# A Fourier filter and a snake MLP on one core: the DFT tables moved into the GpSimd DMA queue, and a weight scaled in eight parts

## Chip, cores and metric

The kernel runs on one core of a Trainium2 chip. The metric is the device time of one execution in microseconds (us). The profile comes from one execution that the hardware profiler recorded; its times are counted from the start of the span.

## What is computed

The input x has 8 batches of 3008 rows by 256 channels. Along the 3008 rows of each batch a real Fourier transform is taken, multiplied with a complex filter, and transformed back. The result goes through an MLP with 2048 hidden channels and the snake activation.

```python
def _attn_ref(x, filt_r, filt_i):
    X = np.fft.rfft(x, axis=1)
    F = (filt_r + 1j * filt_i)[None, :, :]
    Y = X * F
    y = np.fft.irfft(Y, n=x.shape[1], axis=1)
    return y.astype(np.float32)

def _moe_ref(x, w_in, w_out, alpha):      # x: (8 * 3008, 256)
    h = x @ w_in
    s = np.sin(alpha * h)
    g = h + s * s / (alpha + 1e-09)
    return (g @ w_out).astype(np.float32)
```

## The kernel before

The transform of length 3008 = 47 x 64 is done with matrix products, in two steps. Step one is a DFT of length 47, for which 24 frequencies (NK) are kept; step two is a DFT over the 64 residues, folded by symmetry, with one matrix for each of the 24 frequencies. The matrices are constants in device memory. The forward table of step two is `wb` (128 rows by 24 x 128 columns, fp16, 768 KB), the backward tables are `wg` and, with its row halves exchanged and one negated, `wgs` (the same size each). They are cut into chunks of eight frequencies, that is 1024 columns or 256 KB; `s0` = 0, 8, 16 names a chunk.

The program has a prologue and a main loop. The main loop runs over 47 groups `g` of 512 rows of the MLP. In each group, for eight slots `q`, `mlp_in` (L269) makes two blocks of hidden channels (a matrix product, then a sine on ScalarE), `mlp_out` (L283) does a part of the second product of the group before, and `square` (L279) squares the sines on VectorE. The transform of the later batches, 1 to 7, is cut into small pieces that a plan by slots (L413 to 457, `at(slot, f, ...)`) puts between the MLP's pieces: `f1` (step one, result `asb`), `f2x`, `product` with the filter, `f2g` and `f3` (back). Their rearrangements between the steps go through device memory, by DMAs issued on SP.

The prologue does the transform of batch 0, before any MLP work can start, and keeps it on the chip. Its order is written out by hand (L487 to 506):

- `f1_chip` (L151) is step one on the x of batch 0, which arrives in four parts, and `turn1` (L162) turns its result into `bint`;
- `f2x(0, t)` (L201), for t = 0 to 11, multiplies two frequencies each with `wb`;
- `fold_filter(s0, 8)` (L405) copies a chunk of the loaded filter on VectorE to the other half of the partitions;
- `product(0, k, 0)` (L210), for k = 0 to 5, multiplies four frequencies with the filter's real and imaginary parts on VectorE, giving `z` and `t2`, in two buffers each;
- `g_chip(k, half)` (L172) multiplies `z` with `wg` and `t2` with `wgs` on TensorE; k = 0, 1 need chunk 0, k = 2, 3 chunk 8, k = 4, 5 chunk 16;
- `turn2` (L183) and `f3` (L249) finish batch 0; then the first `mlp_in` can start.

`keep_busy(n, zero)` (L388) issues n matrix products whose result is not used. `prep_w_out` (L351) makes `w_out2` out of the loaded `w_out16`: sixteen blocks of 256 columns, each multiplied on VectorE with 1/alpha. The plan has it in four parts of four blocks in slots 6, 8, 10 and 12; `mlp_out` of group 0 reads the result from slot 8 on.

The loads of the prologue stand in two queues. GpSimd's queue holds the loads that also cast fp32 to fp16: x of batch 0 (eight DMAs), the three filter chunks (four DMAs each), w_in (four), x of batch 1 (eight, once `bint` is no longer read, since both share a buffer), and w_out (two). SP's queue holds the tables: a first part of `wb` at once, the rest of `wb` behind the third part of x, and each chunk of `wg` and `wgs` behind the filter chunk that the products ahead of it need. These dependencies are made by `gate` (L123), which makes one DMA's issue wait for an earlier DMA to land.

Of the kernel before, what the change touches and what calls it, by code (L numbers as in the profile page):

```python
# [9 lines left out]
FP16 = mybir.dt.float16  # L10
# [5 lines left out]
MT, R, NK, RP = 47, 64, 24, 32  # L16
# [48 lines left out]
def kernel(  # L65
# [10 lines left out]
    nc = tc.nc  # L76
# [3 lines left out]
    def dram(ap, off, dims):  # L80
        return bass.AP(tensor=ap.tensor, offset=ap.offset + off, ap=dims)
# [3 lines left out]
    wb_d = nc.inline_tensor(wb_np, name="wb_tbl")  # L85
    wg_d = nc.inline_tensor(wg_np, name="wg_tbl")
# [3 lines left out]
    wgs_d = nc.inline_tensor(wgs_np, name="wgs_tbl")  # L90
# [7 lines left out]
    ginpool = ctx.enter_context(tc.tile_pool(name="ginp", bufs=2))  # L98
# [13 lines left out]
    wb = cpool.tile([128, NK * 128], FP16, name="wb")  # L112
    wg = cpool.tile([128, NK * 128], FP16, name="wg")
# [6 lines left out]
    xt, asb, scr1, bint, xs, z, t2, gsb, scr2, gin, yt, vt, po, ot, x_dma, w_in_dma, filter_dma = (  # L120
        {} for _ in range(17))

    def gate(ins, earlier):  # L123

        tc.add_manual_dep(ins.ins, earlier.ins.name, mybir.DependencyInfo(
            mybir.DependencyClass.Sync, mybir.DependencyReason.DATA), reason="order of transfers")

    def load_x(b, parts=2):

        xt[b] = (xbpool if b else vpool).tile([GT, RP, C], FP16, name="xt", tag="xb" if b else "vt")  # L130
        n = RP // parts
        for h in range(parts):
            for p0, p1 in ((0, 80), (80, GT)):
                x_dma[b, h] = nc.gpsimd.dma_start(  # L134
                    out=xt[b][p0:p1, n * h:n * h + n, :],
                    in_=dram(x, (b * S + RP * p0 + n * h) * C, [[RP * C, p1 - p0], [1, n * C]]))
# [203 lines left out]
    def prep_alpha():  # L340
        ps = pso.tile([128, 2, C], FP32, name="psal", tag="po")
        nc.tensor.matmul(out=ps[:, 0, 0:16], lhsT=alpha_r, rhs=ident32, start=True, stop=True)
        nc.vector.tensor_copy(out=alpha_t, in_=ps[:, 0, 0:16])
        nc.vector.tensor_scalar(out=recip, in0=alpha_t, scalar1=1e-9, scalar2=None, op0=ALU.add)
        nc.vector.reciprocal(out=recip, in_=recip)
# [3 lines left out]
                                   in_=moe_w_out[1024 * h:1024 * h + 1024, :].rearrange("(b p) c -> p b c", p=128))  # L349

    def prep_w_out(k):  # L351
        for i in range(4 * k, 4 * k + 4):
            nc.vector.tensor_scalar(out=w_out2[:, i, :], in0=w_out16[:, i, :],  # L353
                                    scalar1=recip[:, i:i + 1], scalar2=None, op0=ALU.mult)

# [32 lines left out]
    def keep_busy(n, src):  # L388

        ps = psh.tile([128, 2, C], FP32, name="idle", tag="ph")  # L390
        for _ in range(n):
            nc.tensor.matmul(out=ps, lhsT=ident[0:src.shape[0]], rhs=src, start=True, stop=True)

    def load_filter(s0, n, earlier=None):

        for f, src in ((0, filt_r), (1, filt_i)):
            first = nc.gpsimd.dma_start(out=fri[0:32, f, s0:s0 + n, :],
                                        in_=dram(src, s0 * C, [[MT * C, 32], [C, n], [1, C]]))
            if earlier is not None and f == 0:
                gate(first, earlier)  # L400
            filter_dma[s0, f] = nc.gpsimd.dma_start(
                out=fri[32:64, f, s0:s0 + n, :],
                in_=dram(src, (MT - s0) * C, [[MT * C, 32], [-C, n], [1, C]]))
# [11 lines left out]
    def at(slot, f, *args):  # L415
        plan.setdefault(int(2 * slot), []).append((f, args))
# [19 lines left out]
    for g in range(NCH - 1):  # L436
# [4 lines left out]
        slots = (4, 6) if len(todo) == 2 else (3, 4, 6, 7) if g == 4 else (3, 4, 5, 6)  # L441
        for q, u in zip(slots, todo):
            at(8 * g + q, f3, *u)
    for k in range(4):
        at(6 + 2 * k, prep_w_out, k)
    for k in range(2):
        at(13, prep_m, k)
    at(14, load_w_in32, 0)
# [10 lines left out]
    with tc.manual_schedule():  # L459
        nc.sync.dma_start(out=wa2, in_=wa2_d.ap())  # L460
        nc.sync.dma_start(out=ident, in_=id_d.ap())
        nc.scalar.dma_start(out=alpha_r, in_=moe_alpha.rearrange("(a p) -> a p", p=128))
        nc.scalar.dma_start(out=ident32, in_=id32_d.ap())
        nc.scalar.dma_start(out=we2, in_=we2_d.ap())
        nc.scalar.dma_start(out=wa, in_=wa_d.ap())
        nc.scalar.dma_start(out=we, in_=we_d.ap())
        nc.sync.dma_start(out=wb[:, 0:8 * 128], in_=wb_d.ap()[:, 0:8 * 128])
        zero = cpool.tile([128, 512], FP16, name="zero")
        nc.vector.memset(zero, 0.0)
        warm = cpool.tile([128, 1], FP32, name="warm")  # L470
        nc.vector.memset(warm, 0.0)
        nc.scalar.activation(out=warm, in_=warm, func=AFT.Sin)
        load_x(0, 4)
        for s0 in (0, 8, 16):
            load_filter(s0, 8, None if s0 else x_dma[0, 1])
        for h in range(2):
            hs = slice(1024 * h, 1024 * h + 1024)
            for cb in range(2):
                w_in_dma[h, cb] = nc.gpsimd.dma_start(out=w_in16[:, cb, hs],
                                                      in_=moe_w_in[128 * cb:128 * cb + 128, hs])  # L480
        wgs = ginpool.tile([128, NK * 128], FP16, name="wgs", tag="gin")
        gate(nc.sync.dma_start(out=wb[:, 8 * 128:], in_=wb_d.ap()[:, 8 * 128:]), x_dma[0, 2])
        for s0 in (0, 8, 16):
            cs = slice(128 * s0, 128 * s0 + 1024)
            gate(nc.sync.dma_start(out=wg[:, cs], in_=wg_d.ap()[:, cs]), filter_dma[s0, 0])
            nc.sync.dma_start(out=wgs[:, cs], in_=wgs_d.ap()[:, cs])
        a_c = vpool.tile([128, 2, NK, 128], FP16, name="a_c", tag="vt")  # L487
        prep_alpha()
        keep_busy(8, zero)
        for k in range(8):  # L490
            f1_chip(k)
            if k % 2:
                keep_busy(2 if k < 7 else 1, zero)
        bint[0] = xbpool.tile([128, NK, C], FP16, name="bint", tag="xb")
        b_c = agpool.tile([128, 2, RP, NK, 4], FP16, name="b_c", tag="ag")
        for f, *args in (
                (turn1, 0), (turn1, 1), (turn1, 2), (f2x, 0, 0), (turn1, 3), (turn1, 4), (f2x, 0, 1),
                (turn1, 5), (turn1, 6), (f2x, 0, 2), (turn1, 7), (fold_filter, 0, 8), (turn1, 8),
                (f2x, 0, 3), (product, 0, 0, 0), (turn1, 9), (f2x, 0, 4), (turn1, 10), (f2x, 0, 5),
                (product, 0, 1, 0), (turn1, 11), (f2x, 0, 6), (keep_busy, 2, zero), (g_chip, 0, 0), (g_chip, 0, 1), (f2x, 0, 7),  # L500
                (fold_filter, 8, 8), (f2x, 0, 8), (keep_busy, 2, zero), (product, 0, 2, 0), (g_chip, 1, 0), (g_chip, 1, 1),
                (f2x, 0, 9), (keep_busy, 2, zero), (product, 0, 3, 0), (f2x, 0, 10), (f2x, 0, 11), (keep_busy, 2, zero), (g_chip, 2, 0), (g_chip, 2, 1),
                (fold_filter, 16, 8), (keep_busy, 2, zero), (product, 0, 4, 0), (g_chip, 3, 0), (g_chip, 3, 1),
                (product, 0, 5, 0), (keep_busy, 2, zero), (g_chip, 4, 0), (g_chip, 4, 1), (keep_busy, 2, zero), (g_chip, 5, 0), (g_chip, 5, 1),
                (keep_busy, 1, zero)):
            f(*args)
        gin[0] = ginpool.tile([4 * NK, RP, C], FP16, name="gin", tag="gin")
        for j in range(4):
            turn2(j)
        load_x(1, 4)  # L510
        load_w_out(0)
        load_w_out(1)
        for i in range(4):
            if i % 2 == 0:
                keep_busy(1, zero)
            f3(i // 2, i % 2)

        for g in range(NCH):
            for q in range(8):
                if g and q == 7:  # L520
                    evict_out(g - 1, 0)
                mlp_in(g, 2 * q)
                if g:
                    mlp_out(g - 1, q, 1)
                for f, args in plan.get(16 * g + 2 * q, ()):
                    f(*args)
                mlp_in(g, 2 * q + 1)
                if g:
                    mlp_out(g - 1, q, 0)
                for f, args in plan.get(16 * g + 2 * q + 1, ()):  # L530
                    f(*args)
                if g and q == 7:
                    evict_out(g - 1, 1)
                    store_out(g - 1, 0, 4, (nc.sync,))
                if q % 2:
                    square(g, q)
        out_last(NCH - 1)
# [28 lines left out]
```

## Time and profile before

| | us |
|---|---|
| median of 3 runs | 833.29 |
| lowest, highest | 833.17, 837.02 |
| the profiled execution | 836.87 |
| its span, first to last instruction | 835.0 |
| last matmul of `g_chip` (L177) starts | 38.35 |
| first matmul of `mlp_in` (L274) | 42.2 |

The parts of the page, for the main loop, by engine and line, costliest first (line, engine, operation, count; then busy time, and mean ns of one; then the idle time before them and what ended it):

```profile
L276 ACT ACTIVATE vt<-ph 128x512 f16<-128x512 f32 x688 | 404.5, 601 | 141.8 <-PE ph L274 136.9
L293 PE MATMUL po<-w_out,vt 128*128 128x256 f16 x2944 | 426.5, 272 | 1.1 <-DVE w_out L353 0.6
L274 PE MATMUL ph<-yt,w_ina 128*128 128x512 f16 x1376 | 399.4, 379 | 0.0
```

How to read the profile: PE is TensorE, PEld its weight loads, DVE is VectorE, ACT is ScalarE, POOL is GpSimd and SP is SyncE; a q behind the name is that engine's queue of instructions. `L177` is line 177 of the kernel. A transfer is shown by the instruction that issues it and by what waits for its landing; the time in between is in the chain of waits as a piece of DMA. The whole main loop is one where TensorE works without a break and ScalarE waits for it.

### The profile page before, as it was taken

The numbers are of one execution on the slowest core, as the hardware profiler recorded it, in microseconds if no ns is written. First come the engines' busy times: TensorE is split into PE (matmuls) and PEld (weight loads), VectorE is DVE, ScalarE is ACT, GpSimd is POOL, SyncE is SP. The second block draws the span as 40 slices with busy tenths as digits, with TensorE's granted clock in tenths as the row PEclk, the third lists the DMA queues.
The fourth block names the chain that finished last, engine by engine and source line by source line (L and its number), as shares of the span: only waits on it lengthen the run. The fifth ranks groups of instructions, "written<-read, shape, count | busy, mean of one in ns | idle before, by whom it ended". The sixth has DMA issues, their size and how long they took to land.

```text
span 835.0 us, 15131 instructions
## 1 busy us (share of the span) xinstructions
PE 816.3 (98%) x6242; PEld 573.1 (69%) x6242; DVE 509.9 (61%) x675; ACT 619.0 (74%) x1156; POOL 35.0 (4%) x65
## 2 busy tenths in 40 slices
PE   7699999999999999999999999999999999999997
PEld 4557776677767776677767776677766777766666
DVE  4586976676466665566655684567655775444442
ACT  5596987787777777788777887777877787766663
POOL 5400000000000000000000000000000000000000
PEclk9999999999999999999999999999999999999999
DMA  9946365424543164612834146331645123310111
GB/s 198 210 75 215 120 169 127 141 76 107 145 107 122 51 156 95 202 31 72 191 99 140 51 105 172 101 102 51 160 118 142 61 93 95 67 51 26 26 52 51
DMA packets 67829, 91.28 MB, mean 109 GB/s; under 512 B 5512, under 2 KB 52376, under 8 KB 66248
## 3 DMA queue, kind: packets, MB, share of 16 engines
q1 hardware_dynamic: 59664, 70.99, 29.5%
q0 software_dynamic: 7568, 19.14, 11.8%
q8 instruction: 49, 0.80, 0.4%
q10 hardware_dynamic: 528, 0.18, 0.1%
q14 instruction: 20, 0.16, 0.1%
HBM read 59.62 MB, written 46.66 MB: 127 GB/s over the span
## 4 chain that ended last, share of the span: by engine, by line
PE 91%; DMA 3%; DVE 3%; ACT 1%; POOL 1%; issue 0%; SPq 0%; POOLq 0%; DVEq 0%
PE po L293 42%; PE ph L274 37%; PE psa L143 3%; PE psy L262 3%; PE psg L234 2%; PE psx L204 2%; DMA fri<-in_filt_r_dram 1%; DMA wgs<-wgs_tbl 1%; PE pe L307 1%; DMA xt<-in_x_dram 1%; DVE vt L281 1%; PE psm L372 0%; ACT vt L276 0%; DVE gin L191 0%; DVE w_ina L385 0%
## 5 line engine op out<-in xcount | busy, mean ns | idle before, releaser
L276 ACT ACTIVATE vt<-ph 128x512 f16<-128x512 f32 x688 | 404.5, 601 | 141.8 <-PE ph L274 136.9
L293 PE MATMUL po<-w_out,vt 128*128 128x256 f16 x2944 | 426.5, 272 | 1.1 <-DVE w_out L353 0.6
L293 PEld LDWEIGHTS <-vt 128*128 128x128 f16 x2944 | 287.4, 98 | 172.2 <-issue 1.1
L274 PE MATMUL ph<-yt,w_ina 128*128 128x512 f16 x1376 | 399.4, 379 | 0.0
L281 DVE TENSOR_TENSOR vt<-vt 128x2048 f16<-128x2048 f16 x188 | 230.1, 1224 | 195.3 <-ACT vt L276 194.4
L274 PEld LDWEIGHTS <-w_ina 128*128 128x128 f16 x1376 | 128.2, 98 | 32.6
L318 DVE COPY ot<-po 128x512 f32<-128x512 f32 x92 | 62.9, 688 | 22.2 <-PE po L293 21.3
L208 ACT CAST xs<-psx 128x512 f16<-128x512 f32 x96 | 56.8, 596 | 7.6 <-PE psx L204 7.4
L144 DVE CAST asb<-psa 96x512 f16<-96x512 f32 x56 | 38.3, 685 | 33.4 <-PE psa L143 30.6
L236 ACT CAST gsb<-psg 128x512 f16<-128x512 f32 x84 | 49.5, 589 | 11.5 <-PE psg L234 10.7
L293 PE MATMUL po<-m_t,yt 128*128 128x256 f16 x368 | 55.2, 273 | 0.0
L267 DVE CAST yt<-psy 128x240 f16<-128x240 f32 (+45 forms) x92 | 32.2, 351 | 32.8 <-ACT yt L264 31.6
L264 ACT CAST yt<-psy 128x376 f16<-128x376 f32 (+46 forms) x127 | 45.9, 362 | 7.5 <-PE psy L262 0.6
L276 ACT ACTIVATE vt<-ph,alpha_t 128x512 f16<-128x512 f32 x64 | 43.7, 703 | 9.4 <-PE ph L274 9.3
L262 PE MATMUL psy<-we,gin 96*128 96x94 f16 x512 | 42.1, 204 | 0.0
L134 POOL DMA_DIRECT2D xt<-in_x_dram x40 | 21.3, 540 | 491.8 <-PE psy L262 300.7
L262 PEld LDWEIGHTS <-gin 96*128 96x128 f16 x512 | 35.6, 97 | 6.9 <-issue 0.5
L293 PEld LDWEIGHTS <-yt 128*128 128x128 f16 x368 | 36.0, 98 | 4.2
L144 ACT CAST asb<-psa 96x512 f16<-96x512 f32 x56 | 32.9, 587 | 8.0 <-PE psa L143 7.7
L217 DVE TENSOR_TENSOR z<-xs,fri 128x1024 f16<-128x1024 f16 x48 | 33.0, 687 | 8.3 <-ACT xs L208 4.6
L274 PE MATMUL ph<-yt,w_in 128*128 128x512 f16 x128 | 37.8, 379 | 0.2 <-ACT yt L264 0.2
L204 PE MATMUL psx<-bint,wb 128*128 128x256 f16 x192 | 36.8, 276 | 0.4 <-ACT bint L169 0.2
(69 smaller groups left out, 383.7 us busy)
## 6 DMA issues: line engine op xcount, KB each, us to landing
scr<-asb SPq DMA_DIRECT2D x14, 768.0 KB
bint<-scr SPq DMA_DIRECT2D x21, 512.0 KB
scr<-gsb SPq DMA_DIRECT2D x21, 512.0 KB
out_dram<-ot SPq DMA_DIRECT2D x31, 320.0 KB
xt<-in_x_dram POOLq DMA_DIRECT2D x12, 640.0 KB, 7.7
gin<-scr SPq DMA_DIRECT2D x7, 768.0 KB
out_dram<-ot SPq DMA_DIRECT2D x16, 256.0 KB
gin<-scr SPq DMA_DIRECT2D x7, 576.0 KB
```

Of the source, the lines that this page charges most:

```text
L144: (nc.vector.tensor_copy if u % 2 else nc.scalar.copy)(out=asb[b][:, 2 * u:2 * u + 2, :], in_=ps)
L204: nc.tensor.matmul(out=ps[:, i, :], lhsT=wb[:, 128 * (2 * t + i):128 * (2 * t + i) + 128], rhs=bint[b][:, 2 * t + i, :], start=True, stop= ...
L208: nc.scalar.copy(out=xs[b, t // 2][:, t % 2 * 2:t % 2 * 2 + 2, :], in_=ps)
L217: nc.vector.tensor_tensor(out=z[k], in0=xs[b, k], in1=fri[:, 0, k4, :], op=ALU.mult)
L236: nc.scalar.copy(out=gsb[b][:, 2 * t:2 * t + 2, :], in_=ps)
L262: nc.tensor.matmul(out=ps[:, t, :], lhsT=gin[b][:, 4 * a + t, 128 * cb:128 * cb + 128], rhs=we if b else we2, start=True, stop=True)
L264: (nc.vector.tensor_copy if G == 0 and cb else nc.scalar.copy)(out=yt[g][:, cb, :, lo:lo + n], in_=ps[:, :, 0:n])
L274: nc.tensor.matmul(out=ph, lhsT=(w_in16 if g < 4 else w_ina)[:, cb, 128 * jb:128 * jb + 128], rhs=yt[g][:, cb], start=(cb == 0), stop=(cb ...
L276: nc.scalar.activation(out=vt[g][:, jb, :], in_=ph, func=AFT.Sin, scale=alpha_t[:, jb:jb + 1] if g < 4 else 1.0)
L281: nc.vector.tensor_tensor(out=v4, in0=v4, in1=v4, op=ALU.mult)
L293: nc.tensor.matmul(out=po[g, h][:, i, :], lhsT=vt[g][:, k, ts] if k < 16 else yt[g][:, k - 16, t], rhs=w_out2[:, k, :] if k < 16 else m_t[ ...
L318: nc.vector.tensor_copy(out=ot[g][:, 2 * h:2 * h + 2, :], in_=po[g, h])
```

## The change

The seven table loads on SP and their gates go. The same loads are issued by GpSimd instead, between the filter chunks: behind filter chunk 0 the rest of `wb` and the chunk 0 of `wg` and `wgs`, behind chunks 8 and 16 their `wg` and `wgs`. The loads of w_in come after all of these. The first part of `wb` stays on SP. `prep_w_out` is cut into eight parts of two blocks in slots 6, 6.75, 7.5 and so on to 11.25. One of the two idle matrix products ahead of `g_chip(5, ...)` goes.

```diff
     def prep_w_out(k):
-        for i in range(4 * k, 4 * k + 4):
+        for i in range(2 * k, 2 * k + 2):
             nc.vector.tensor_scalar(out=w_out2[:, i, :], in0=w_out16[:, i, :],
                                     scalar1=recip[:, i:i + 1], scalar2=None, op0=ALU.mult)
...
-    for k in range(4):
-        at(6 + 2 * k, prep_w_out, k)
+    for k in range(8):
+        at(6 + 0.75 * k, prep_w_out, k)
...
         load_x(0, 4)
+        wgs = ginpool.tile([128, NK * 128], FP16, name="wgs", tag="gin")
         for s0 in (0, 8, 16):
+            cs = slice(128 * s0, 128 * s0 + 1024)
             load_filter(s0, 8, None if s0 else x_dma[0, 1])
+            if s0 == 0:
+                nc.gpsimd.dma_start(out=wb[:, 8 * 128:], in_=wb_d.ap()[:, 8 * 128:])
+            nc.gpsimd.dma_start(out=wg[:, cs], in_=wg_d.ap()[:, cs])
+            nc.gpsimd.dma_start(out=wgs[:, cs], in_=wgs_d.ap()[:, cs])
         for h in range(2):
             hs = slice(1024 * h, 1024 * h + 1024)
             for cb in range(2):
                 w_in_dma[h, cb] = nc.gpsimd.dma_start(out=w_in16[:, cb, hs],
                                                       in_=moe_w_in[128 * cb:128 * cb + 128, hs])
-        wgs = ginpool.tile([128, NK * 128], FP16, name="wgs", tag="gin")
-        gate(nc.sync.dma_start(out=wb[:, 8 * 128:], in_=wb_d.ap()[:, 8 * 128:]), x_dma[0, 2])
-        for s0 in (0, 8, 16):
-            cs = slice(128 * s0, 128 * s0 + 1024)
-            gate(nc.sync.dma_start(out=wg[:, cs], in_=wg_d.ap()[:, cs]), filter_dma[s0, 0])
-            nc.sync.dma_start(out=wgs[:, cs], in_=wgs_d.ap()[:, cs])
...
-                (product, 0, 5, 0), (keep_busy, 2, zero), (g_chip, 4, 0), (g_chip, 4, 1), (keep_busy, 2, zero), (g_chip, 5, 0), (g_chip, 5, 1),
+                (product, 0, 5, 0), (keep_busy, 2, zero), (g_chip, 4, 0), (g_chip, 4, 1), (keep_busy, 1, zero), (g_chip, 5, 0), (g_chip, 5, 1),
```

## The prediction

> **What bounds the kernel now.** The page's first part says that TensorE is busy nearly throughout:
>
> ```profile
> PE 816.3 (98%) x6242; PEld 573.1 (69%) x6242; DVE 509.9 (61%) x675; ACT 619.0 (74%) x1156; POOL 35.0 (4%) x65
> ```
>
> So only a stretch in which it waits can give time back. The list of who waited for whom, cut to 0 to 90 us, finds those waits:
>
> ```profile
> PE psg L177 <- DMA wgs<-wgs_tbl: 4.8, 3, 1.9
> ...
> PE psg L177 <- DMA wg<-wg_tbl: 1.4, 2, 1.0
> ...
> PE po L293 <- DVE w_out L353: 0.6, 1, 0.6
> ```
>
> The columns are total, times and longest, in us. The backward tables cost 6.2 us of TensorE's own waiting, all in g_chip. The chain of waits between 14 and 45 us, in order of time (start, length, what), says why they are late:
>
> ```profile
> 14.44 10.77 DMA fri<-in_filt_r_dram
> ...
> 25.23 0.32 SPq L485
> 25.55 0.05 issue
> 25.60 10.61 DMA wgs<-wgs_tbl
> 36.20 0.04 issue
> 36.24 1.00 PE psg L177 x15
> 37.24 0.43 PE idle L392 x2
> 37.67 0.91 PE psg L177 x16
> 38.58 0.02 issue
> 38.61 0.70 DVE b_c L180
> ```
>
> The last pair of tables is issued only when the third filter chunk has landed (25.21), and needs 10.6 us for 256 KB. The table of stretches tells what it shares the DMA engines with (second column from the right: DMA share, last: GB/s):
>
> ```profile
> 0.00:12.00 12.00, 8.56 (x64) 4.73 (x64) 3.54 (x11) 3.99 (x8) 6.99 (x17) 1.00 0.85 166
> 12.00:24.00 12.00, 7.95 (x92) 6.01 (x91) 8.05 (x14) 8.55 (x18) 6.18 (x11) 0.97 1.18 227
> 24.00:30.00 6.00, 5.35 (x43) 3.74 (x41) 4.75 (x6) 4.69 (x9) 1.93 (x2) 0.78 1.03 209
> 30.00:36.00 6.00, 2.81 (x36) 2.22 (x36) 2.81 (x5) 2.15 (x4) 3.94 (x8) 1.00 1.09 247
> 36.00:45.00 9.00, 7.77 (x90) 5.56 (x90) 5.12 (x9) 5.34 (x11) 1.83 (x2) 1.00 1.23 189
> 45.00:50.00 5.00, 4.49 (x38) 2.78 (x38) 3.90 (x6) 4.52 (x8) 0.00 (x0) 1.00 0.20 27
> ```
>
> From 12 to 45 us the DMA engines are full. So what sets the prologue is the order in which bytes are moved: w_in (20.8 to 24.1) and x of batch 1 (from 29.25) are issued while the last tables are still outstanding, though nobody needs them before 42.2 and 50.7. From 50 us on DMA is idle until 58. GB/s times length gives bytes moved: 1.99 MB by 12 us, 4.72 by 24, 5.97 by 30, 7.45 by 36, 9.15 by 45.
>
> **The tables.** Seven SP issues and their two kinds of gate go; SP's next work is the store at 58.21, so nothing is queued behind them. GpSimd gets seven issues more. Its x issues take a mean 540 ns, so 7 x 0.54 = 3.8 us, in a queue that waits 4.0 us ahead of the filter, 2.1 and 2.0 inside it and 4.0 before x of batch 1: hidden as long as eight DMAs are under way, since the built program lets each GpSimd DMA wait for the one eight before it. Then the order in the queue alone counts. From issue sizes (x 1504 KB, the first part of wb, small loads: 1.93 MB together; every step after that 512 KB or 0.524 MB) the running sum after each step, and when the curve above reaches it: filter 0 2.45 MB; wb rest 2.98, 16.4 us; pair 0 3.50, 18.6; filter 8 4.03, 21.0; pair 8 4.55, 23.3; filter 16 5.08, 25.7; pair 16 5.60, 28.2; w_in first half 6.12, 30.6; second 6.65, 32.8; x of batch 1 8.19, 39.9; w_out 9.24, 45.5. From last byte to waiter I add 1.5 us, an estimate: x (1.93 MB) is passed before 12 us and its last matmul started at 13.08.
>
> Against the needs: wb at 17.9 (it came at 18.84). Pair 0 at 20.1; TensorE stood ready at 21.47 and 22.07, its first g_chip began in earnest at 23.2, so 1.1 us come back there. Filter 8 at 22.5; VectorE reaches its fold after the second product, 23.2, not 23.94. Pair 8 at 24.8, before TensorE gets there. Filter 16 at 27.2: this is late next, since VectorE would reach its fold after product 3 at about 27.3 (29.00 before, less the 1.6 that g_chip(1) gains). Call the start of this fold F. Behind it stand products 4 and 5, then g_chip(5). From the rows of the trace: fold to product 1.35 (23.94 to 25.29), two products 2.63 (32.59 to 34.54+0.68), then 0.04 and a last g_chip 1.06 (37.51 to 38.35+0.22). The last ends at F + 5.1 = 32.4, against 38.57. Pair 16 at 29.7 is ahead of g_chip(4) at about F + 2.7 = 30.0. Gain 6.2.
>
> What is moved back: w_in's halves land at 32.1 and 34.3; the first mlp_in moves from 42.2 to 36. x of batch 1 is complete at 41.4, first used at 44.5. The first half of w_out (8.72 MB) lands near 44, first scaling 49.9. No wait is added if the curve holds.
>
> It need not hold: it was made by two queues. The nearest row of one queue alone is 36 to 45 us, when SP's tables are in: 189 GB/s. Then filter 16 lands at 12 + 3.09/0.189 + 1.5 = 29.8 and the last g_chip ends at 34.9: gain 3.7. That row is x and w_out with casting, w_out in short rows, while the tables are plain copies in long rows; so I take the curve, and keep 3.7 as the low end. The high end is VectorE's own pace: F one microsecond earlier, 7.2.
>
> [...]
>
> **The scaling of w_out.** Still 16 operations of 0.86/4 = 0.21 us, so VectorE's total is the same; they come in twos and are done by slot 11.25, not 12. TensorE's waits around it are 0.59 (at 70.03, the last scaling) and 0.27 (at 57.60, for asb behind four scalings): the gain is at most 0.86. But four scalings now come ahead of the square at 63.04, which pushes it and two asb copies back by up to 0.86, where VectorE's idle time is 0.57: a loss is possible up to about the same. I take 0.4 gained, with -0.9 to +0.9 kept.
>
> **keep_busy.** One matmul of 0.22 fewer before g_chip(5). It lies under the wait for product 5 (g_chip(4) ends a microsecond after F + 2.7, the product comes at F + 4.0), so nothing; 0.2 gained without that cover.
>
> **The sum.** 6.2 + 0.4 = 6.6 off the profiled execution, whose 836.87 (span 835.0) is 3.6 above the median of 833.29. TensorE's granted clock was 0.998 and steady, and after 50 us DMA has slack, so the excess may well lie in the prologue's transfers, and then an ordinary run has less waiting to give. All of it there: gain 3.0, 830.3. None: 826.7. I take the middle: 4.8 gained, **828.5**, own range 826 to 830.5.
>
> **Rivals.** (a) *One queue feeds more slowly.* For: 189 GB/s in the only stretch with GpSimd alone. Against: 204 GB/s at 3 to 6 us with hardly anything beside it, and short rows. Gain 3.7 + 0.4 - 1.8 = 2.3: 831.0, within 0.5%. Chance 0.20.
>
> (b) *The wait is not there in an ordinary run*, since the tables mostly come in time, and VectorE's chain sets the end anyway: gain about the 0.4 of w_out, 832.9. For: two of three runs are 3.6 shorter than the profile. Against: even then 3 of the 6.6 are left. Chance 0.10.
>
> (c) *Slower: GpSimd cannot keep its queue full.* Filter 16 must land after 33.5 for F + 5.1 to pass 38.57, which is 3.09 MB in 20 us: below 155 GB/s the change loses. For: two issues beside VectorE's fold took twice their time:
>
> ```profile
> 19.57 1.21 POOL L401 DMA_DIRECT2D fri<-in_filt_i_dram  x1 [1.96 <-DMA fri<-in_filt_i_dram]
> 20.76 0.56 POOL L479 DMA_DIRECT2D w_in<-in_moe_w_in_dram  x1
> ...
> 24.10 1.18 POOL L479 DMA_DIRECT2D w_in<-in_moe_w_in_dram  x1 [0.33 <-DMA fri<-in_filt_i_dram]
> ```
>
> Both end when the fold does (19.40 + 1.22; 23.94 + 1.22). Against: three folds at 0.6 each are 1.9 us in 20, and eight DMAs (over 1 MB) cover them; the slowest 3 us of the queue alone still moved 164 GB/s (39 to 42). At 135 GB/s the last g_chip ends at F = 36.4 + 5.1 = 41.5, 2.9 late, and half of w_out lands at 63.4 where 59.0 is needed: 4.4, less VectorE's 1.4 of idle time. 833.3 + 5.9 = 839. Chance 0.10.
>
> [...]
>
> (d) *The scaling takes back its 0.9* while the tables give their share: 6.2 - 1.8 - 0.9 = 3.5, 829.8. Chance 0.07.
>
> **Chances and range.** The forecast has 0.53. 0.5% is 4.2 us, about what a measurement of this kernel can tell: faster is below 829.1. The forecast lies there for most of its range; together with gains above it 0.56. (a), (b), (d) and the rest of the forecast are no change: 0.33. Slower: 0.11. The range must hold the forecast, the full 7.2 + 0.9 and (a), (b), (d): 825 to 834; outside is (c).
>
> **What will show it.** In the profile of the changed kernel: wgs no longer in the chain of waits; the third fold starts near 27 and waits for the filter's DMA or not at all; the last psg ends near 32 to 33 (38.57 before); the first mlp_in near 36, without a wait for w_in; no wait at L353. The prediction is wrong if filter 16 lands after 30, if a gap of DMA shows between 12 and 30 us (queue starved), if w_in or w_out is waited for, or if asb waits grow between 50 and 65 us by more than the two waits that go.

## The result, and the profile after

The changed kernel took 830.23 us in the median of 15 runs (828.98 to 833.54), the kernel before 834.73 us in the median of 15 (832.81 to 839.18). The ratio is 0.9947, 95% interval 0.9931 to 0.9962: 4.5 us, half a percent, faster. The forecast was 828.5 us and a gain of 4.8.

The profiled execution of the changed kernel took 829.13 us, with a span of 827.2, against 836.87 and 835.0. These two differ by more than the medians do; why is shown below.

Who waited for whom on TensorE, 0 to 90 us, in the changed kernel (total, times, longest, in us), the list's head:

```profile
PE psal L342 <- DMA ident<-id_tbl: 3.1, 1, 3.1
PE psa L156 <- DMA xt<-in_x_dram: 1.1, 2, 0.6
PE psg L177 <- DVE t L219: 0.7, 2, 0.4
```

The waits for wg and wgs, 6.2 us before, are gone, and so is the one for the scaling of w_out; g_chip now waits only for VectorE's product. `psal` and `psa` in this list belong to the start and to step one. VectorE's own order of time in the changed kernel (start, length, instruction, and in brackets the idle time before it):

```profile
25.67 0.68 DVE L219 TENSOR_TENSOR t<-xs,fri 128x1024 f16<-128x1024 f16 x1
26.40 1.22 DVE L407 COPY fri<-fri 64x4096 f16<-64x4096 f16 x1
27.76 0.69 DVE L217 TENSOR_TENSOR z<-xs,fri 128x1024 f16<-128x1024 f16 x1
...
29.57 0.69 DVE L219 TENSOR_TENSOR t<-xs,fri 128x1024 f16<-128x1024 f16 x1
31.36 0.69 DVE L180 CAST b_c<-psg 128x512 f16<-128x512 f32 x1 [1.11 <-PE psg L177]
```

The third fold starts the moment VectorE has finished the product ahead of it, without a wait for the filter. What sets the end of the prologue in this profile is VectorE's chain; in the two later profiles of the changed kernel the third fold waited for the filter, by 1.56 and 0.30 us. The last matmul of g_chip starts at 31.11 (38.35 before), the first mlp_in at 34.99 (42.23 before). The table of stretches of the changed kernel (third column from the right: granted TensorE clock; then DMA share and GB/s):

```profile
12.00:24.00 12.00, 10.13 (x123) 7.61 (x122) 9.57 (x15) 10.21 (x22) 8.86 (x16) 1.00 1.16 251
24.00:30.00 6.00, 5.46 (x64) 3.97 (x62) 5.82 (x9) 5.16 (x11) 5.12 (x8) 1.00 1.10 214
30.00:36.00 6.00, 5.26 (x66) 3.70 (x64) 3.65 (x8) 3.73 (x9) 2.34 (x4) 1.00 1.09 213
36.00:45.00 9.00, 8.23 (x68) 4.97 (x66) 7.88 (x11) 7.84 (x15) 1.04 (x2) 1.00 1.23 189
45.00:50.00 5.00, 5.00 (x36) 2.69 (x35) 4.74 (x11) 5.00 (x11) 0.00 (x0) 1.00 0.03 4
```

In this profile one queue alone moved 251 GB/s from 12 to 24 us, where two moved 227 before; two later profiles of the changed kernel have 212 and 246. The bytes are the same and are done at nearly the same time, about 45 us; their order is another.

### The profile page after: what moved, and what is told of

It reads as the page before. It is cut to its first block, busy times and chain, and to the rows that moved or that the text cites. A ratio compares the mean times of both kernels' runs of the same rounds, so it can differ in the third digit from the quotient of the medians.

```text
span 827.2 us, 15124 instructions
## 1 busy us (share of the span) xinstructions
PE 814.4 (98%) x6241; PEld 570.7 (69%) x6241; DVE 509.7 (62%) x675; ACT 618.3 (75%) x1156; POOL 38.6 (5%) x72
## 4 chain that ended last, share of the span: by engine, by line
PE 88%; DVE 2%; DMA 1%; ACT 0%; issue 0%; DVEq 0%
PE po L293 42%; PE ph L274 37%; PE psa L143 3%; PE psy L262 2%; PE psg L234 2%; PE psx L204 2%; DMA w_in<-in_moe_w_in_dram 1%; PE pe L307 1%; DVE w_ina L385 0%; DVE vt L281 0%; DVE t L224 0%; DVE z L226 0%; DVE t L221 0%; DVE ot L318 0%; DVE z L217 0%; DVE yt L267 0%
## 5 line engine op out<-in xcount | busy, mean ns | idle before, releaser
L262 PE MATMUL psy<-we,gin 96*128 96x94 f16 x512 | 42.2, 205 | 0.0
L293 PEld LDWEIGHTS <-yt 128*128 128x128 f16 x368 | 35.9, 98 | 4.3
```

Source lines behind the costliest of these rows:

```text
L262: nc.tensor.matmul(out=ps[:, t, :], lhsT=gin[b][:, 4 * a + t, 128 * cb:128 * cb + 128], rhs=we if b else we2, start=True, stop=True)
L293: nc.tensor.matmul(out=po[g, h][:, i, :], lhsT=vt[g][:, k, ts] if k < 16 else yt[g][:, k - 16, t], rhs=w_out2[:, k, :] if k < 16 else m_t[ ...
```

## The experiments

The theory was that the order in which the prologue's bytes are moved pays, by letting the tables come ahead of w_in and of x of batch 1. The rivals were the split scaling, the gates, the single queue as such, and the clock. Ratios are against the kernel before on the same chip.

| kernel | median, us | ratio, 95% interval | first mlp_in in its profile |
|---|---|---|---|
| tables_only | 831.66 | 0.9959 (0.9942 to 0.9976) | 36.66 |
| w_out_only | 834.17 | 0.9998 (0.9982 to 1.0015) | 43.06 |
| w_in_behind | 832.88 | 0.9969 (0.9954 to 0.9984) | 38.97 |
| no_gates | 834.72 | 0.9997 (0.9983 to 1.0011) | 40.82 |
| w_in_ahead | 837.90 | 1.0039 (1.0024 to 1.0054) | 40.85 |
| sp_early | 831.57 | 0.9958 (0.9941 to 0.9975) | 36.27 |
| warm | 836.38 | 1.0014 (0.9998 to 1.0031) | 42.11 |
| wb_behind_x | 829.73 | 0.9947 (0.9928 to 0.9966) | 35.05 |
| after_again | 830.88 | 0.9956 (0.9941 to 0.9970) | 39.67 |
| after_third | 830.87 | 0.9948 (0.9929 to 0.9968) | 35.53 |
| before_again | 836.82 (one run) | | 42.21 |

**The parts by themselves.** First the table loads alone:

```diff
 # the changed kernel, with
+        for i in range(4 * k, 4 * k + 4):          # prep_w_out
+    for k in range(4):
+        at(6 + 2 * k, prep_w_out, k)
+                ... (g_chip, 4, 1), (keep_busy, 2, zero), (g_chip, 5, 0) ...
```

> The changed kernel with the scaling of w_out in four parts and both idle products ahead of g_chip(5), as before: the table loads alone are changed. Theory (the order of the bytes pays): in the profile the first mlp_in starts at 35 to 35.5 us as in the changed kernel (34.99), and the time is 3.5 to 4.5 us below the kernel before. Rival (the scaling's split makes much of the gain): under 2.5 us below the kernel before.

And the scaling alone:

```diff
 # the kernel before, with
+        for i in range(2 * k, 2 * k + 2):          # prep_w_out
+    for k in range(8):
+        at(6 + 0.75 * k, prep_w_out, k)
```

> The kernel before with only the scaling of w_out in eight parts. Theory: TensorE's waits at 57.6 and 70.0 us of before (0.27 + 0.59) go, a gain of 0.4 to 0.9 us at most, within the scatter of the runs; the first mlp_in stays near 42. Rival (the split is a large part): a gain of 2 us or more. Second rival (it takes back what it gives, as squares and asb copies come later): no gain in the part of the span behind the first mlp_in, 792.8 us before.

The tables alone keep 3.4 us (1 - 0.9959 of 834.97). That is just short of the 3.5 to 4.5 expected, and the first mlp_in came at 36.66, not at 35 to 35.5; this profile has a granted clock of 0.86 from 12 to 24 us. The scaling alone cannot be told from nothing. TensorE's wait for it does go, as the page's group of those matmuls shows in the changed kernel:

```profile
L293 PE MATMUL po<-w_out,vt 128*128 128x256 f16 x2944 | 426.5, 273 | 0.6 <-DVE ot L318 0.6
```

Before, the idle time was 1.1 us, 0.6 of it for w_out at L353. How much of this reaches the end is read from the span behind the first mlp_in, in all profiles: 792.6 to 793.3 us, mean 792.8, in seven profiles with four parts, and 792.0 to 793.2, mean 792.4, in six with eight. The difference is the forecast's 0.4, but the two groups overlap and scatter by 0.7 and 1.2 us; no run proves it.

**Order, gates or queue.** The kernel before, with w_in held back:

```diff
+            wg_dma = nc.sync.dma_start(out=wg[:, cs], in_=wg_d.ap()[:, cs])
+            gate(wg_dma, filter_dma[s0, 0])
...
+        gate(w_in_dma[0, 0], wg_dma)       # w_in issued here, behind the tables
```

> The kernel before, tables on SP with their gates, but the loads of w_in wait until the last chunk of wg has landed (and so x of batch 1, behind them in the queue, comes later too). Theory (what the tables shared the DMA engines with was the cost): the last pair lands by 30 to 32 us, the first mlp_in starts at 35 to 38, gain 3 us or more, without any table in GpSimd's queue. Rival (the gates, that is the late issue, were the cost): the first mlp_in stays at 40 us or later, gain under 1.5 us.

```diff
 # the kernel before, with
-        gate(nc.sync.dma_start(out=wb[:, 8 * 128:], in_=wb_d.ap()[:, 8 * 128:]), x_dma[0, 2])
+        nc.sync.dma_start(out=wb[:, 8 * 128:], in_=wb_d.ap()[:, 8 * 128:])
...
-            gate(nc.sync.dma_start(out=wg[:, cs], in_=wg_d.ap()[:, cs]), filter_dma[s0, 0])
+            nc.sync.dma_start(out=wg[:, cs], in_=wg_d.ap()[:, cs])
```

> The kernel before, tables on SP, without the gates: the tables are issued as soon as SP gets to them and w_in stays where it was in GpSimd's queue. Theory (order of bytes): 2.1 MB of tables now come beside x and the first filter chunk, so step one ends some 3 to 6 us later than 13.95 us, and no wait for a table is left; the first mlp_in starts at 37 to 42, between the two kernels or no better than before. Rival (the gates were the cost): it starts near 35 as in the changed kernel.

```diff
 # the changed kernel, with the loads of w_in moved
         for s0 in (0, 8, 16):
...
+            if s0 == 16:
+                for h in range(2): ...   # the four loads of w_in
             nc.gpsimd.dma_start(out=wg[:, cs], in_=wg_d.ap()[:, cs])
```

> The changed kernel with one thing moved: in GpSimd's queue the four loads of w_in stand ahead of the third pair of tables instead of behind it. Same queue, same bytes, no gates. Theory (the order of the bytes is what pays): 1.05 MB at about 0.21 MB/us puts the third pair some 5 us later, to about 33 us; g_chip(4) waits for it, the first mlp_in moves from 35 to 37 to 39, the time is 2 to 4 us above the changed kernel's. Rival (one queue without gates is what pays, whatever its order): no change against the changed kernel, the first mlp_in at 35 to 36.

Taking the gates away and nothing else gains nothing: the tables then run beside x and the first filter chunk, and VectorE's first fold starts at 23.64, not 19.40. Holding w_in back, and with it x of batch 1 behind it in the queue, gains 2.6 us, and TensorE waits for the last pair no more. Theory had expected 3 us or more and the first mlp_in at 35 to 38; 2.6 and 38.97 lie between theory and rival. It stops short of the changed kernel because the first pair now is what comes late. The chain of waits of w_in_behind:

```profile
14.37 0.32 SPq L480
14.69 0.05 issue
14.74 9.71 DMA wgs<-wgs_tbl
24.46 0.04 issue
24.50 1.00 PE psg L177 x15
...
26.81 1.71 PE psg L177 x16
```

The gate of a pair waits for the real part of its filter chunk. So `wgs` of pair 0 is issued at 14.74, while filters 8 and 16 are issued around it, and it takes 9.7 us for 256 KB. Behind this wait the granted clock falls, to 0.72 from 24 to 30 us, and the second g_chip takes 1.71 us, not 0.9. In the changed kernel, where pair 0 stands ahead of filter 8, TensorE finds it there at 20.66.

Putting w_in ahead of the third pair, in the same queue and without a gate, costs 7.0 us in the medians against the changed kernel run beside it (837.90 and 830.88), and so more than the whole gain. Its waits of TensorE and its stretches:

```profile
PE psg L177 <- DMA wg<-wg_tbl: 3.1, 1, 3.1
...
PE psg L177 <- DMA wgs<-wgs_tbl: 0.9, 1, 0.9
```

```profile
30.00:36.00 6.00, 3.19 (x27) 2.79 (x27) 0.75 (x2) 1.17 (x2) 3.50 (x6) 0.68 1.07 250
36.00:45.00 9.00, 8.24 (x78) 5.82 (x77) 5.97 (x11) 5.72 (x11) 0.43 (x1) 0.83 1.17 178
```

The wait for the third pair is 4.0 us, and behind it the granted clock falls to 0.68 and 0.83: the matmuls of the last two g_chip follow each other at 0.107 us instead of 0.055. Against the first profile of the changed kernel the first matmul with `wgs` in g_chip(4) comes 3.9 us later (33.02, not 29.11) and the last matmul of g_chip 5.5 (36.60, not 31.11); the other 1.6 us are the half clock. Theory's direction and wait were right, its size was not (2 to 4 us and the first mlp_in at 37 to 39 were expected): the clock was left out, and this profile, at 835.12 the fastest of the 12 runs, does not show what the median has beyond that. So "one queue without gates" is not what pays; its order is.

The last question was whether the order needs that one queue:

```diff
 # w_in_behind, with each pair let go earlier
-            gate(wg_dma, filter_dma[s0, 0])
+            gate(wg_dma, x_dma[0, 3] if s0 == 0 else filter_dma[s0 - 8, 1])
```

> As w_in_behind (tables on SP, w_in behind the last wg), but each pair of tables is let go one step earlier: pair 0 when the last part of x has landed, pair 8 and pair 16 when the filter chunk two steps ahead of their use has landed. Two queues, nearly the order of need. Theory (order of bytes, in whichever queue): the first mlp_in at 35 to 38, the time within 1.5 us of the changed kernel's, below w_in_behind's 832.9. Rival (it takes one queue to get the order): no better than w_in_behind.

No need of one queue shows: with the tables on SP, two queues and gates in nearly the order of need, the ratio is 0.9958 (0.9941 to 0.9975), which cannot be told from the 0.9948 (0.9929 to 0.9968) of the changed kernel run beside it.

**The clock.** In the kernel before, TensorE also fell to half clock, behind its wait for the first pair: the granted clock was 0.81 from 22 to 24 us and 0.56 from 24 to 27, with matmuls of g_chip 0.107 us apart there too.

```diff
 # the kernel before
-                (f2x, 0, 6), (keep_busy, 2, zero), (g_chip, 0, 0), ...
+                (f2x, 0, 6), (keep_busy, 14, zero), (g_chip, 0, 0), ...
```

> The kernel before with 14 instead of 2 idle products ahead of g_chip(0), so that TensorE doesn't stand still while it waits for the first pair of tables (its granted clock was 0.56 from 24 to 27 us of before). Theory (the last pair's landing at 36.2 us sets the end of the prologue): the clock stays higher from 20 to 27 us, the first mlp_in stays at 41 to 43 and the time is within 1 us of the kernel before. Rival (a good part of the gain is that TensorE no longer falls to half clock): the time falls by 2 us or more.

The stretches of the kernel before and then of warm:

```profile
20.00:24.00 4.00, 1.71 (x13) 1.07 (x11) 3.19 (x6) 2.62 (x6) 2.38 (x4) 0.90 1.22 201
24.00:30.00 6.00, 5.35 (x43) 3.74 (x41) 4.75 (x6) 4.69 (x9) 1.93 (x2) 0.78 1.03 209
```

```profile
20.00:24.00 4.00, 4.00 (x28) 2.22 (x27) 3.72 (x5) 2.76 (x6) 1.80 (x3) 1.00 1.25 216
24.00:30.00 6.00, 4.52 (x49) 3.38 (x48) 4.94 (x6) 4.50 (x9) 3.87 (x5) 1.00 1.11 236
30.00:36.00 6.00, 4.30 (x36) 3.39 (x36) 2.01 (x4) 2.25 (x4) 3.51 (x7) 0.72 1.09 246
```

The clock is 1.00 up to 30 us, and the time is not lower: the ratio of 1.0014 is 1.2 us above the kernel before (within 1 us was expected), with 1 in its interval. The waits for the tables remain, and the clock falls behind the next of them (0.90 and 1.74 us around one product, then 0.72 from 30 to 36 us). In both kernels it is back before the last `wgs` is there (first used at 36.24 and 36.12 us), and the first mlp_in starts at 42.23 and 42.11: here the half clock lies under the wait for the last pair. In all three profiles of the changed kernel the clock is 1.00 in every stretch up to 50 us.

**Why two executions differ.** The changed kernel was profiled twice more, the kernel before once more.

> The changed kernel itself once more, for a second profile and as the measure for the two others. Theory (executions differ in the prologue alone): the span behind the first mlp_in is again 792 to 793 us, whatever the whole span is. Rival (they differ all along): it moves with the span.

> The changed kernel a third time, beside the two others. Theory (its executions differ in how fast the DMA engines move the prologue's bytes): the first mlp_in moves with the GB/s between 12 and 30 us (251 and 214 in the first profile with mlp_in at 34.99; 212 and 173 in the second with 39.67), and the rest of the span is again 792 to 793 us. Rival: it differs with equal GB/s.

> The kernel before itself once more, for a second profile. Theory (executions differ in the prologue alone, in when the tables land): the span behind the first mlp_in is again 792 to 793 us, and the first mlp_in lies between 38 and 43 us with the waits for wgs longer or shorter by the same amount. Rival: the first mlp_in is at 42 as before and the rest differs.

The second profile of the changed kernel (after_again), TensorE's waits, the stretches, and VectorE's second and third fold:

```profile
PE psg L177 <- DVE z L217: 2.4, 2, 1.8
PE psg L177 <- DMA wgs<-wgs_tbl: 1.8, 2, 1.2
...
PE psx L204 <- DMA wb<-wb_tbl: 1.0, 1, 1.0
```

```profile
12.00:24.00 12.00, 8.72 (x113) 6.66 (x110) 8.50 (x13) 9.68 (x21) 6.46 (x13) 1.00 1.11 212
24.00:30.00 6.00, 4.84 (x53) 3.51 (x51) 3.72 (x5) 4.84 (x11) 4.27 (x7) 1.00 1.06 173
```

```profile
25.66 1.22 DVE L407 COPY fri<-fri 64x4096 f16<-64x4096 f16 x1 [3.02 <-DMA fri<-in_filt_i_dram]
...
31.07 1.22 DVE L407 COPY fri<-fri 64x4096 f16<-64x4096 f16 x1 [1.56 <-DMA fri<-in_filt_i_dram]
```

The same program moved 212 and 173 GB/s where it had moved 251 and 214; wb, the filter and the tables all came late, and the first mlp_in at 39.67. The third profile has 246 and 220 GB/s and 35.53. The span behind the first mlp_in was 792.2, 792.0 and 792.1. So these three executions differ in the prologue alone, and there with the rate of the DMA engines. Why that rate differs stays open. In the second profile GpSimd itself stood still for 2.8 us, until the eighth DMA back (wb) had landed. The DMA engines moved 253 GB/s meanwhile (17.1 to 20.0 us); they had been slow before it, with 107 GB/s from 13.5 to 14.7 us, against 229 in the first profile:

```profile
16.56 0.57 POOL L480 DMA_DIRECT2D wg<-wg_tbl  x1 [0.31 <-DMA fri<-in_filt_i_dram]
19.96 0.55 POOL L481 DMA_DIRECT2D wgs<-wgs_tbl  x1 [2.84 <-DMA wb<-wb_tbl]
```

For the kernel before the second profile has the first mlp_in at 42.21, with 5.6 us of waits for the tables; its half clock comes later, from 33 to 36 us (0.50), and changes nothing in that start either. From its median one can work out where the first mlp_in usually is: 834.73, less 1.9 outside the span, less 792.8, is 40.0; both profiles show it 2 us late. In the changed kernel it is 830.23 - 1.9 - 792.4 = 35.9. Both figures are worked out; no profile shows the kernel before at its median.

**A further step.** The first part of wb, behind x:

```diff
 # the changed kernel
-        nc.sync.dma_start(out=wb[:, 0:8 * 128], in_=wb_d.ap()[:, 0:8 * 128])
         load_x(0, 4)
+        nc.gpsimd.dma_start(out=wb[:, 0:8 * 128], in_=wb_d.ap()[:, 0:8 * 128])
```

> The changed kernel with the first part of wb (256 KB) moved as well, from SP, where it runs beside x of batch 0, to GpSimd's queue right behind x. Theory (in the changed kernel nothing but VectorE's and TensorE's chain behind x is left in the prologue): x is complete about 0.8 us earlier (0.26 MB at 0.3 MB/us), the first mlp_in comes 0.5 to 0.8 us earlier, the time is 0 to 1 us below the changed kernel's. Rival (filter or tables set the pace again as soon as x comes earlier): the third fold waits for the filter, and nothing is gained.

x is complete 0.4 us earlier (0.8 was expected, with 0.3 MB/us; from 6 to 12 us the changed kernel moved 206 GB/s), and the first fold starts 0.4 us earlier (18.18). But the third starts at 26.45, after 0.56 idle, against 26.40. VectorE gets there sooner, while the last filter DMA is issued at 21.00 (20.93 in the changed kernel). That the fold waited for this filter is likely; the profile names no releaser. The ratio, 0.9947 over five runs, cannot be told from the changed kernel's, and no version tried here is shown to beat it.

## Why the prediction was right

**The tables.** The step named filter 16 as what is late next, usable at 27.2 by the curve of bytes, with VectorE at its third fold at F = 27.3. F was 26.40, 31.07 and 26.91 in three profiles. In the first, VectorE did not wait there, and F came 0.9 us early: the step had left the first fold where it was, but this started at 18.59 without a wait, not at 19.40. The gain, 7.24 us (38.57 to 31.33), is the step's high end. In the third, 0.30 us of waiting for the filter were left. The second shows rival (a)'s slow rate: its F is later than the 29.8 of the low end, and its gain of 2.6 us lies under the low end's 3.7. As the same program had the faster rate in the two others, this is a matter of the execution and not of the queue.

From F to the end of the last g_chip the sum had 5.1 us; measured 4.93 (31.11 + 0.22 - 26.40), 4.93 and 4.95. Pair 0 was expected at 20.1; GpSimd's queue waited for it, as the eighth DMA back, until 19.38 in the first profile. TensorE did not wait for w_in in any of the three; neither for x of batch 1 nor for w_out.

Of the two rates between which the step chose, the curve's was the better one. No slower rate of one queue as such shows: from 12 to 24 us the traces have 251, 212 and 246 GB/s in three profiles of one queue, and 227 and 226 in the two of the kernel before; sp_early, with two queues, agrees by its time (0.9958, and 0.9948 for the changed kernel). That casting and short rows made the row of 189 GB/s low was the author's assumption; no run moved the same loads without them.

Three readings on the way were not right, though little hung on them. The gate of the last pair waits for the real part of the third filter chunk, not for the whole of it. By the curve's own last row, 27 GB/s from 45 us on, w_out is done at 48.3, not at 45.5. And the granted clock was not steady: the stretch from 24 to 30 us has 0.78.

**The scaling.** 0.4 was taken out of -0.9 to 0.9; the spans behind the first mlp_in differ by 0.4 in the mean, within their scatter. Rival (d), a loss of 0.9 there, shows in no profile's mean.

**From the profile to the median.** Here the text chose the middle between two readings of the 3.6 us by which the profile exceeded the median. That the gain of 4.5 us comes so near to the forecast's 4.8 is in part luck. The median was one of three runs, 833.29; that of 15 is 834.73, so the excess was 2.1 us. All of it seems to have lain in the prologue: the usual first mlp_in of the kernel before is worked out as 40.0, not 42.2. By that reading the sum gives 6.6 - 3.6 = 3.0 with the median of three runs, and 6.6 - 2.1 = 4.5 with that of 15. Half of too large an excess came out nearly the same. The time itself, 830.23, is 1.7 above the forecast of 828.5, and 1.4 of this is the other median. The terms worked out from the medians are 4.1 for the prologue (40.0 to 35.9) and 0.4 behind it.

**Rivals (b) and (c).** (b), no wait in an ordinary run, is refuted by w_in_behind and tables_only, which gain without touching the rest. (c), that GpSimd cannot keep its queue full, has its sign in after_again (2.8 us without an issue), but what ended it was a landing, and it began 1.7 us before VectorE's fold did (17.13 and 18.82). GpSimd's issues beside a fold took at most 1.25 us, where the x loads of the kernel before take a mean 0.54, and in the first profile, where one of them took 0.99, TensorE waited for no table. So the traces show longer issues beside a fold, and no run shows that they cost time here.

**What the forecast left out.** The clock. It was 1.00 in the prologue of the changed kernel, so it made no difference there, but in w_in_ahead's profile it added 1.6 us to the 3.9 of the wait.

## What to carry to other kernels

While the DMA engines are full, as here from 12 to 45 us (a DMA share of 1.03 to 1.23 in the first profiles of both kernels), look not at which queue a load is in but at which bytes are ahead of it: write the running sum of bytes in the order of issue beside the times of need, and move what nobody needs yet behind what is waited for. A wrong order in one queue cost 7 us here, while two queues with gates that nearly keep the order could not be told from one (ratios of 0.9958 and 0.9948). And where one profile is above the median, find out which stretch holds the excess before the whole of a wait is counted as gain.

## What the runs showed of the hardware

The rate at which the same loads in the same order were moved varied between executions, from 212 to 251 GB/s over 12 us and from 173 to 220 over the 6 us behind, and in its three profiles the changed kernel's span varied with it (827.2, 831.7 and 827.6 us), ahead of the first mlp_in alone (34.99, 39.67 and 35.53, with 792.2, 792.0 and 792.1 behind it).

TensorE's granted clock fell behind short waits, though not behind all of them. In w_in_ahead it was 0.68 from 30 to 36 us, behind 4.0 us of waits with one product between them, the longer 3.12, and the matmuls that followed stood 0.107 us apart instead of 0.055. In the kernel before it was 0.56 from 24 to 27 us, behind 1.05 and 1.13 us of waits around one product. But in the second profile of the kernel before (before_again), waits of 0.77 and 1.31 us around the same product left the clock at 1.00 until 30 us. The waits were for DMAs in the first two cases, and in no_gates for VectorE's products (1.74 and 0.38 us, with 0.72 from 24 to 30 us behind them). Which wait brings the clock down was not shown.
